# Where the tiles of a two-stage expert kernel start within a partition of SBUF

## The chip, the cores and the metric

The kernel runs on one core of a Trainium2 chip. The metric is the device time of one execution in microseconds (us): before the change the median of three runs is 1172.26 us (1172.18 to 1172.64).

## The reference

A causal convolution over 7 tokens, with softmaxed taps for each of 8 heads, then two feed-forward layers with different gates. All is float32.

```
w = softmax(weight)                                  # 8 heads x 7 taps
x = sum over k of w[head, k] * x_padded[token + k]   # x: 2 x 4096 tokens x 192
h = x @ w_in;  x = (h * clip(h + 3, 0, 6) / 6) @ w_out             # 192 -> 2048 -> 192
h = x @ w_in2; x = where(h > 0, h, exp(min(h, 0)) - 1) @ w_out2    # 192 -> 2048 -> 192
```

## The kernel before

The 8192 tokens are cut into 16 blocks of 512 columns, features on the partitions. Of each layer's 2048 hidden features, 128 make one *slot*: 2 layers x 16 blocks x 16 feature groups f = 512 slots. A slot has three steps.

- **First product** (`mm1`, L471 to L493): five matmuls of 512 columns put the sum h into one PSUM bank. To keep float32 accuracy with operands rounded to fp32r, weights and activations are split into a high and a low part, so `wi*h`, `wi*l` and `wi*r` (high, low, and both parts of the 64 features beyond 128) meet `opA`, `opB`, `opC` and `opD`.
- **Gate** (`gate`, `split_g`, L495 to L512): ScalarE makes u from h, VectorE makes g, ScalarE rounds it to `gh`, VectorE makes the rest `gl`.
- **Second product** (`mm2`, L516 to L532): five matmuls of `gh` and `gl` with slices of `wo` add into two PSUM banks over the 16 groups; the last slice of the five loads only 66 of 128 weight columns, save in the last group.

The second product runs LAG = 4 slots behind the first. The first 32 slots use all 128 rows of TensorE (`stream(ALL, ...)`, L793). After them two streams, one on partitions 0 to 63 and one on 64 to 127, are issued in turn, 8 matmuls apart (L805 to L812), so that two matmuls of 64 rows run side by side. In this form a slot has 9 first and 10 second matmuls.

Everything else is threaded between the slots by `run_jobs` (L578): decoding and splitting of the weights (`decode`, `split_w`), the convolution (`conv`), operand splits (`split_y`), sums and stores. Its meters count planned work and know nothing of addresses. Only the convolution of the first two blocks is done by TensorE (`taps_tensor`, L281): for k = 0 to 6 a plain float32 matmul of 256 columns reads the tile `xT` from 4k bytes past its start.

Tiles come from pools that are laid out in a partition one behind the other in the order of L90 to L97: `const`, `stage`, `xin`, `cv`, `tmp`, `gp`, `yp`, `op`. A tile's start is rounded up to 32 bytes only. As the small constants (`ident`, `taps` and the like) and the tiles of `cv` have odd sizes, the later pools start where these leave off. Of the starts the table gives the remainder in bytes, before the change; the tiles with several buffers have the same one in all.

| tile | size | start modulo 2048 | modulo 512 |
|---|---|---|---|
| `wi`, `wo` (weights) | 8192, 24576 | 128 | 128 |
| `opA` to `opD`, `gh`, `gl`, `g`, `u`, `xw`, `cw`, `y0`, `yr`, `s1` | 2048 | 1088 | 64 |
| `raw`, `y2`, `z` | 4096 | 1920 | 384 |
| `x_sb`, `xr_sb` | 2048, 1024 | 1920, 896 | 384 |
| `xT0` (two buffers) | 2096 | 1920, 1984 | 384, 448 |

One slot's weights of `wi` start at f x 512 bytes into the tile, those of `wo` at f x 1536 bytes plus 0, 512 or 1024. So modulo 2048 the weights of a matmul start at 128, 640, 1152 or 1664, by f.

Of the kernel before, what the change touches and what calls it, by code (L numbers as in the profile page):

```python
# [8 lines left out]
F32 = mybir.dt.float32  # L9
# [8 lines left out]
P = 128  # L18
# [37 lines left out]
def conv_moe_moe2(ctx: ExitStack, tc: tile.TileContext, x, weight, w_in1, w_out1, w_in2, w_out2, out):  # L56
# [19 lines left out]
    H, K = weight.shape  # L76
# [13 lines left out]
    const = ctx.enter_context(tc.tile_pool(name="const", bufs=1))  # L90
    stage = ctx.enter_context(tc.tile_pool(name="stage", bufs=3))
    xin = ctx.enter_context(tc.tile_pool(name="xin", bufs=2))
    cv = ctx.enter_context(tc.tile_pool(name="cv", bufs=1))
    tmp = ctx.enter_context(tc.tile_pool(name="tmp", bufs=2))
    gp = ctx.enter_context(tc.tile_pool(name="gp", bufs=LAG + 1))
    yp = ctx.enter_context(tc.tile_pool(name="yp", bufs=RA - 1))
    op = ctx.enter_context(tc.tile_pool(name="op", bufs=3))  # L97
    ps_h = ctx.enter_context(tc.tile_pool(name="ps_h", bufs=3, space=PSUM))
    ps_o = ctx.enter_context(tc.tile_pool(name="ps_o", bufs=5, space=PSUM))

    w_in = (w_in1, w_in2)
    w_out = (w_out1, w_out2)
    wi = [{n: const.tile([P, FF], F32R, name=f"wi{l}{n}") for n in ("h", "l", "r")} for l in range(2)]
    wo = [const.tile([P, NF, 2 * D], F32R, name=f"wo{l}") for l in range(2)]

    ident = const.tile([P, P], F32, name="ident")
    relay = const.tile([1, 1], F32, name="relay")
    three = const.tile([P, 1], F32, name="three")
    taps = const.tile([P, 2, K], F32, name="taps")


    def word(raw, i):
# [69 lines left out]


    def load_taps():
        raw = const.tile([H, K], F32, name="traw")
        nc.scalar.dma_start(raw, weight)
        e = const.tile([H, 2, P], F32, name="heads")
        nc.gpsimd.memset(e, 1.0)
        for part, pat, base in ((0, [[1, P]], 0), (1, [[0, 2], [1, R]], P)):
            v = e[:, part, :]  # L190
            nc.gpsimd.affine_select(out=v, in_=v, pattern=pat, compare_op=ALU.is_ge, fill=0.0,
                                    base=base, channel_multiplier=-G)
            nc.gpsimd.affine_select(out=v, in_=v, pattern=[[-st, n] for st, n in pat], compare_op=ALU.is_ge, fill=0.0,
                                    base=G - 1 - base, channel_multiplier=G)
        mx = const.tile([H, 1], F32, name="mx")
        vec.tensor_reduce(out=mx, in_=raw, axis=AX.X, op=ALU.max)
        vec.tensor_scalar(out=raw, in0=raw, scalar1=mx, scalar2=None, op0=ALU.subtract)
        ex = const.tile([H, K], F32, name="etap")
        act.activation(ex, raw, AF.Exp)
        sm = const.tile([H, 1], F32, name="sm")  # L200
        vec.tensor_reduce(out=sm, in_=ex, axis=AX.X, op=ALU.add)
        vec.tensor_scalar(out=sm, in0=sm, scalar1=1e-9, scalar2=None, op0=ALU.add)
        vec.reciprocal(sm, sm)
        vec.tensor_scalar(out=ex, in0=ex, scalar1=sm, scalar2=None, op0=ALU.mult)
        yield
        pt = ps_h.tile([P, 2, K], F32, name="pt", tag="h")
        for part in range(2):
            nc.tensor.matmul(pt[:, part, :], e[:, part, :], ex, start=True, stop=True)
        vec.tensor_copy(taps, pt)
        yield  # L210
# [471 lines left out]
    with tc.manual_schedule():  # L682
        tp, tr = load_taps(), transposes(0)
        make_identity(nc, ident)
        load_rows(0)
        next(tp)
        ahead(0)
        nc.gpsimd.memset(three, 3.0)
        next(tp)
        next(tr)  # L690
        next(tr)
        for k in range(K):
            vec.tensor_scalar(out=diag[k], in0=ident, scalar1=taps[:, 0, k:k + 1], scalar2=None, op0=ALU.mult)
        for _ in range(2):
            next(main)
        r = conv_r(0)
        while ready[0] < FIRST0:
            next(weights)
            next(r, None)
        drain(r)  # L700
        load_rows(1)
        drain(main)
# [6 lines left out]
    for b in range(2, NBLK):  # L709
        e = at[0, b, 0] - 2  # L710
        if b <= RA:
            t = at[0, b - 1, 0]
            if b > 2:
                t, e = t - 2, e + (b < RA)
            else:
                t += NF // 2
        else:
            t = at[0, b - 1, 0] - 8
            e = at[0, b - 1, NF - 1]
        job(feed(b), 1, t - 8, t - 7)  # L720
        job(whole(squares(b), conv(b)), 2 + CONV, t, e, WORK["conv"])
    for b in range(NBLK):
        e = at[1, b, 0]
# [120 lines left out]
```

## Time and profile before

| | |
|---|---|
| median of three runs | 1172.26 us |
| the profiled execution's own time | 1171.86 us |
| its span, first to last instruction | 1170.1 us |
| mean granted TensorE clock | 1.000 of full (2.4 GHz) |
| TensorE busy | 1159.8 us, 99% |
| VectorE busy | 918.7 us, 79% |
| ScalarE busy | 933.1 us, 80% |

The profile has one row per TensorE weight load (PEld) and per matmul (PE). Matmuls overlap in their pipeline, so the time that one costs is the distance between the starts of two, and not its own length. A plain float32 matmul leaves two records, an fp32r one leaves one.

### The profile page before, as it was taken

What the parts mean: (1) busy time and instruction counts of PE and PEld (TensorE: products, weight loads), DVE (VectorE), ACT (ScalarE), POOL (GpSimd) and SP (SyncE); (2) the same over time, 40 slices, a digit from 0 to 9 for tenths busy, and PEclk for the clock granted to TensorE, in tenths of its full rate; (3) what the DMA queues carried; (4) which work ended last, traced back from release to release, by engine and by line L of the source; (5) the groups of instructions that cost most, each with busy time, mean ns of one, the idle gap of its engine ahead of it and who ended that gap; (6) DMA issues with size and microseconds to landing.
All of it is one profiled execution on the core that took longest, in us unless ns stands there. A gap on an engine that the chain in (4) does not pass through costs nothing.

```text
span 1170.1 us, 25136 instructions
## 1 busy us (share of the span) xinstructions
PE 1159.8 (99%) x9507; PEld 1098.6 (94%) x9507; DVE 918.7 (79%) x1560; ACT 933.1 (80%) x1685; POOL 44.5 (4%) x490
## 2 busy tenths in 40 slices
PE   8999999999999999999999999999999999999998
PEld 6778999999999999999999999999999998878777
DVE  8997999988977968778686787968767666677765
ACT  6876777778878787887878778787786888888886
POOL 0000000000000000000000000000000000000000
PEclk9999999999999999999999999999999999999999
DMA  6422011010010100101000010100000000000001
GB/s 181 108 68 41 19 42 46 29 28 1 2 28 1 29 1 5 25 1 28 2 15 15 1 29 1 23 7 1 15 2 15 2 9 7 15 15 15 12 7 26
DMA packets 105370, 26.80 MB, mean 23 GB/s; under 512 B 96416, under 2 KB 104096, under 8 KB 105248
## 3 DMA queue, kind: packets, MB, share of 16 engines
q1 hardware_dynamic: 104960, 24.99, 10.1%
q8 instruction: 74, 1.21, 0.4%
q14 instruction: 48, 0.39, 0.1%
q10 hardware_dynamic: 288, 0.20, 0.1%
HBM read 18.87 MB, written 6.29 MB: 22 GB/s over the span
## 4 chain that ended last, share of the span: by engine, by line
PE 97%; DVE 1%; ACT 1%; issue 0%; ACTq 0%; DVEq 0%
PE p L530 50%; PE h L487 47%; DVE acc L50 0%; DVE xw L50 0%; ACT u L50 0%; DVE wi0r L50 0%; DVE cw L50 0%; ACT xw L50 0%; DVE diag L50 0%; ACT opC L50 0%; ACT L50 0%; DVE wo L50 0%; ACT gh L50 0%; ACT opD L50 0%; PE pso L432 0%
## 5 line engine op out<-in xcount | busy, mean ns | idle before, releaser
L530 PE MATMUL p<-gh,wo 64*128 64x512 f32 (+1 forms) x2978 | 625.5, 393 | 0.0
L50 DVE SCALAR_TENSOR_TENSOR g<-u,h 128x512 f32<-128x512 f32 x512 | 349.8, 683 | 214.7 <-ACT u L50 210.8
L530 PE MATMUL p<-gl,wo 64*128 64x512 f32 (+2 forms) x1985 | 503.2, 390 | 0.0
L530 PEld LDWEIGHTS p<-gh,wo 64*128 64x128 f32 (+1 forms) x2978 | 460.0, 185 | 15.5
L50 DVE TENSOR_TENSOR gl<-g,gh 128x512 fp32r<-128x512 f32 x512 | 349.9, 683 | 2.9 <-ACT gh L50 2.4
L50 ACT CAST gh<-g 128x512 fp32r<-128x512 f32 x512 | 311.2, 608 | 11.2 <-DVE g L50 11.0
L530 PEld LDWEIGHTS p<-gl,wo 64*128 64x128 f32 (+1 forms) x1985 | 309.4, 161 | 10.8 <-DVE gl L50 0.4
L50 ACT ACTIVATE u<-h,three 128x512 f32<-128x512 f32 x256 | 175.9, 687 | 120.4 <-PE h L487 116.9
L50 ACT ACTIVATE u<-h 128x512 f32<-128x512 f32 x256 | 152.6, 596 | 66.7 <-PE h L487 65.8
L487 PE MATMUL h<-opA,wi1h 64*128 64x512 f32 x512 | 194.9, 396 | 0.0
L487 PE MATMUL h<-opA,wi1l 64*128 64x512 f32 x512 | 194.6, 396 | 0.0
L487 PE MATMUL h<-opB,wi1h 64*128 64x512 f32 x512 | 192.3, 390 | 0.0
L487 PE MATMUL h<-opA,wi0h 64*128 64x512 f32 (+1 forms) x476 | 180.3, 396 | 0.5 <-ACT opA L50 0.4
L487 PE MATMUL h<-opA,wi0l 64*128 64x512 f32 (+1 forms) x476 | 179.9, 395 | 0.0
L487 PE MATMUL h<-opB,wi0h 64*128 64x512 f32 (+1 forms) x476 | 178.8, 391 | 0.0
L50 ACT ACTIVATE u<-u 128x512 f32<-128x512 f32 x256 | 161.8, 632 | 8.4
L487 PE MATMUL h<-opD,wi1r 64*128 64x512 f32 x384 | 147.1, 393 | 0.0
L487 PE MATMUL h<-opC,wi1r 64*128 64x512 f32 x384 | 146.3, 390 | 0.0
L487 PE MATMUL h<-opC,wi0r 64*128 64x512 f32 (+1 forms) x366 | 139.6, 391 | 0.6 <-ACT opC L50 0.6
L487 PE MATMUL h<-opD,wi0r 64*128 64x512 f32 (+1 forms) x366 | 140.2, 393 | 0.0
L50 DVE SCALAR_TENSOR_TENSOR acc<-xT,taps,acc 128x256 f32<-128x256 f32 (+1 forms) x180 | 105.4, 601 | 0.1
L487 PEld LDWEIGHTS h<-opA,wi1h 64*128 64x128 f32 x512 | 94.2, 184 | 6.6 <-DVE g L50 1.6
(89 smaller groups left out, 1215.4 us busy)
## 6 DMA issues: line engine op xcount, KB each, us to landing
raw<-in_moe_w_out_dram SPq DMA_DIRECT2D x16, 384.0 KB, 3.4
out_dram<-z SPq DMA_DIRECT2D x180, 32.0 KB, 1.6
raw<-in_moe_w_in_dram SPq DMA_DIRECT2D x7, 512.0 KB, 4.3
x_sq<-in_x_dram SPq DMA_DIRECT2D x112, 32.0 KB, 2.2
raw<-in_moe_w_in_dram SPq DMA_DIRECT2D x8, 256.0 KB, 4.0
xr_sq<-in_x_dram SPq DMA_DIRECT2D x56, 32.0 KB, 2.2
x_sb<-in_x_dram SPq DMA_DIRECT2D x4, 128.0 KB, 3.8
raw<-in_moe_w_in_dram SPq DMA_DIRECT2D x4, 128.0 KB, 3.5
```

The costliest lines, as they stand in the source:

```text
L50: return fn(*args, **kw)
L487: mm = nc.tensor.matmul(h, k, m[half], start=low and i == 0, stop=high and i == len(todo) - 1)
L530: nc.tensor.matmul(p[:n, cols], k[:, :n], m[half, cols], start=first and not end and k is not w0l, stop=last and end == 1 and cols.stop == NB)
```

## The change

No instruction is added, taken away or moved: each engine executes the same operations on the same tiles in the same order with the same waits. Two tiles that nobody uses are put ahead, of 384 bytes in `const` and of 320 bytes in `cv`, and the small constants go to a pool `few` of their own behind `op`.

```diff
     op = ctx.enter_context(tc.tile_pool(name="op", bufs=3))
+    few = ctx.enter_context(tc.tile_pool(name="few", bufs=1))
...
+    const.tile([P, 96], F32, name="gap0")
+    cv.tile([P, 80], F32, name="gap1")
     wi = [{n: const.tile([P, FF], F32R, name=f"wi{l}{n}") for n in ("h", "l", "r")} for l in range(2)]
     wo = [const.tile([P, NF, 2 * D], F32R, name=f"wo{l}") for l in range(2)]
 
-    ident = const.tile([P, P], F32, name="ident")
-    relay = const.tile([1, 1], F32, name="relay")
-    three = const.tile([P, 1], F32, name="three")
-    taps = const.tile([P, 2, K], F32, name="taps")
+    ident = few.tile([P, P], F32, name="ident")
+    relay = few.tile([1, 1], F32, name="relay")
+    three = few.tile([P, 1], F32, name="three")
+    taps = few.tile([P, 2, K], F32, name="taps")
```

The scratch tiles of `load_taps` (`traw`, `heads`, `mx`, `etap`, `sm`) move from `const` to `few` in the same way. The starts after the change:

| tile | start modulo 2048 | modulo 512 |
|---|---|---|
| `wi`, `wo` | 512 | 0 |
| `opA` to `opD`, `gh`, `gl`, `g`, `u`, `xw`, `cw`, `y0`, `yr`, `s1` | 0 | 0 |
| `raw`, `y2`, `z` | 512 | 0 |
| `x_sb`, `xr_sb` | 512, 1536 | 0 |
| `xT0` (two buffers) | 832, 896 | 320, 384 |

## Rows read from the trace of the kernel before

**Rows 1.** The page: busy time, share of the span, instructions of each engine.

```profile
PE 1159.8 (99%) x9507; PEld 1098.6 (94%) x9507; DVE 918.7 (79%) x1560; ACT 933.1 (80%) x1685; POOL 44.5 (4%) x490
```

**Rows 2.** The page: the chain that ended last, by engine and by line.

```profile
PE 97%; DVE 1%; ACT 1%; issue 0%; ACTq 0%; DVEq 0%
PE p L530 50%; PE h L487 47%; DVE acc L50 0%; DVE xw L50 0%; ACT u L50 0%; DVE wi0r L50 0%; DVE cw L50 0%; ACT xw L50 0%; DVE diag L50 0%; ACT opC L50 0%; ACT L50 0%; DVE wo L50 0%; ACT gh L50 0%; ACT opD L50 0%; PE pso L432 0%
```

**Rows 3.** Waits: the waiter, its releaser, us in total, times, the longest.

```profile
PE pt L208 <- DVE etap L50: 3.9, 1, 3.9
PE psx L244 <- DMA x_sb<-in_x_dram: 0.5, 1, 0.5
...
DVE g L50 <- ACT u L50: 210.8, 292, 3.5
ACT u L50 <- PE h L487: 182.7, 289, 2.2
```

**Rows 4.** Windows by stage (start, full rows, two streams, end), columns in line one.

```profile
core 0: us, PE busy (x) PEld busy (x) DVE busy (x) ACT busy (x) POOL busy (x), PEclk, DMA share, GB/s
0.00:31.00 31.00, 25.27 (x107) 20.14 (x107) 25.17 (x68) 22.07 (x52) 2.18 (x14) 1.00 0.68 174
31.00:103.00 72.00, 72.00 (x309) 56.47 (x310) 67.50 (x125) 56.48 (x102) 0.00 (x0) 1.00 0.29 74
103.00:1160.00 1057.00, 1057.00 (x9059) 1017.93 (x9059) 823.00 (x1363) 851.75 (x1527) 42.33 (x476) 1.00 0.08 15
1160.00:1170.10 10.10, 5.55 (x38) 4.04 (x34) 3.02 (x6) 2.78 (x6) 0.00 (x0) 0.95 0.13 40
```

**Rows 5.** Chain in order of time, full-row slots: start, length, what.

```profile
32.56 1.17 PE h L487 x5
...
34.88 1.17 PE h L487 x5
...
37.21 1.17 PE h L487 x5
...
46.52 1.17 PE h L487 x5
```

**Rows 6.** PE in order of time, one full-row slot: start, length, matmul.

```profile
60.31 0.40 PE L487 MATMUL h<-opA,wi0h 128*128 128x512 f32 x1
...
62.18 0.62 PE L530 MATMUL p<-gl,wo 128*128 128x512 f32 x2
62.64 0.40 PE L487 MATMUL h<-opA,wi0h 128*128 128x512 f32 x1
...
64.51 0.62 PE L530 MATMUL p<-gl,wo 128*128 128x512 f32 x2
64.97 0.40 PE L487 MATMUL h<-opA,wi0h 128*128 128x512 f32 x1
```

**Rows 7.** PE in order of time, convolution taps of block 1, in two windows.

```profile
17.40 1.24 PE L287 MATMUL psc<-xT,diag 128*128 128x256 f32 x5
...
17.40 5.99 PE L287 MATMUL psc<-xT,diag 128*128 128x256 f32 x27
```

**Rows 8.** PE in order of time, matmuls of 256 columns near the end.

```profile
1163.34 0.40 PE L530 MATMUL p<-gh,wo 64*128 64x256 f32 x2
...
1163.93 0.28 PE L530 MATMUL p<-gl,wo 64*128 64x256 f32 x1
```

More of the change, by code (lines that the diff above doesn't have):

```diff
@@ L184, in load_taps @@
     def load_taps():
-        raw = const.tile([H, K], F32, name="traw")
+        raw = few.tile([H, K], F32, name="traw")
         nc.scalar.dma_start(raw, weight)
-        e = const.tile([H, 2, P], F32, name="heads")
+        e = few.tile([H, 2, P], F32, name="heads")
         nc.gpsimd.memset(e, 1.0)
@@ L194, in load_taps @@
                                     base=G - 1 - base, channel_multiplier=G)
-        mx = const.tile([H, 1], F32, name="mx")
+        mx = few.tile([H, 1], F32, name="mx")
         vec.tensor_reduce(out=mx, in_=raw, axis=AX.X, op=ALU.max)
         vec.tensor_scalar(out=raw, in0=raw, scalar1=mx, scalar2=None, op0=ALU.subtract)
-        ex = const.tile([H, K], F32, name="etap")
+        ex = few.tile([H, K], F32, name="etap")
         act.activation(ex, raw, AF.Exp)
-        sm = const.tile([H, 1], F32, name="sm")
+        sm = few.tile([H, 1], F32, name="sm")
         vec.tensor_reduce(out=sm, in_=ex, axis=AX.X, op=ALU.add)
```

## The prediction

> **What bounds the kernel now.** I read four views. The page's busy times come first: TensorE is busy for 1159.8 of 1170.1 us, VectorE and ScalarE for about 80% [rows 1]. A busy share alone does not make a bound, so the chain that ended last is next. It runs through TensorE for 97%: half of that the second product (L530), nearly all of the rest the first (L487) [rows 2]. The waits point the same way. TensorE's longest is 3.9 us, once, at the start. VectorE waits 210.8 us for ScalarE's u, and ScalarE waits 182.7 us for a matmul's h, that is for TensorE [rows 3]. Last, the windows by stage: from 31 to 1160 us TensorE has no idle time at all, at a granted clock of 1.00. VectorE is busy for 823 of the 1057 us in the long stage and ScalarE for 852 [rows 4]. So only two things can move the time: the rate of a matmul, and the 41 us before and after (0 to 31 and 1160 to 1170).
>
> **The change part by part.** No instruction comes, goes or moves. What may change is the duration of an instruction, because its operands start elsewhere. I go through the places in order of their weight.
>
> *Matmuls at the full rate.* In the stage of full rows seven slot starts at 32.56, 34.88, ..., 46.52 give 13.96 us for six slots, 2.327 us each, or 232.7 ns for each of ten matmuls [rows 5]. In the two streams 9059 records in 1057 us are 116.7 ns apart, and as two run side by side this is 233.4 ns for a pair [rows 4]. Ideal for 512 columns at 2.4 GHz is 213.3 ns, so each costs 20 ns more, and the question of this case is whether these 20 ns hang on the addresses. The number of such units is 9059 / 2 + 309 = 4840 [rows 4]. One ns on each is therefore 4.84 us on the kernel.
>
> Three observations bear on it.
>
> First, the part of an address that is a multiple of 512 bytes makes no difference. From one slot to the next f changes, and with it the weights' start modulo 2048 goes through 128, 640, 1152 and 1664, while the moving operands stay at 1088. The slots still come 2.32 or 2.33 us apart each time [rows 5]. What the change alters for weights is a shift by 384 bytes, from remainder 128 to 0 modulo 512, and for moving operands from 64 to 0. Of that, only the part within 512 bytes is not tried out by the trace.
>
> Second, small misalignment costs next to nothing where the trace has it. The taps read `xT` from 4k bytes past its start, so from seven different places modulo 32. Their records are 215.9 ns apart: (5.99 - 1.24) / 22 [rows 7]. They stream two clocks per column, 256 columns in the 213.3 ns ideal, so the whole excess there, misalignment included, is 2.6 ns. The weights of these (`diag`) lie at 64 modulo 512. This is the nearest row to the question, at half the column rate.
>
> Third, the 20 ns follow other things. Five matmuls of 256 columns come 118 ns apart, (1163.93 - 1163.34) / 5 [rows 8], against 106.7 ideal: 11 ns excess for half the columns. And where the matmuls around a load of 66 columns stand, two take 0.46 us, while the eight others of the slot take 1.87 us [rows 6]: 230 against 233.75 ns. So the excess grows with the streamed columns and shrinks by about 7 ns for 62 columns less of weights. Neither row needs an address to explain it, but reads of weights and of moving data that disturb each other would fit the second.
>
> Bounds from these rows: at best the excess falls to that of the taps, 233.4 - 215.9 = 17.5 ns, times 4840 = 85 us less. At worst the part that goes with the weight load, 7 ns x 128 / 62 = 14 ns, is paid twice: 14 x 4840 = 68 us more. I take 0, by the taps, where starts off any multiple of 32 stay within 2.6 ns, and by the slots that repeat to 0.01 us for every position of the weights.
>
> The Trainium skill has a rule on each side here. "TensorE: Matmul & The Clock Gate", section "Wait — 56ns, not 53.3ns?", gives 215.7 ns between warm matmuls of 512 columns; this trace differs with 233.4 ns, and by that rule some 17.7 ns are there to be won by whatever causes them. "SBUF — State Buffer", section "Who interferes with whom", says that TensorE reads weights and moving data through independent ports and waits on nobody; by it the second bound cannot arise, though the 66-column rows above do not quite agree.
>
> *VectorE and ScalarE.* Their tiles move by the same few bytes. In the long stage they would have to grow by 1057 / 823 = 1.28 and 1057 / 852 = 1.24 before they set the rate [rows 4]. Their work is hidden behind TensorE there. If that cover went, each 1% on VectorE would be 8 us; the cover is 234 us deep. I count 0.
>
> *The start.* Up to 31 us VectorE is busy for 25.2 us, TensorE for 25.3 us of 31 [rows 4], and 5.7 us of TensorE are idle: 3.9 of them wait for the taps (`etap`) and 0.5 for the first `x_sb` [rows 3]. The tiles of the taps move from one odd place to another. Landing of `x_sb` and `raw` at 0 instead of 384 modulo 512 could move a transfer by a tenth or two. Bounds: 0.5 us less if the wait for `x_sb` goes, 0.5 us more if it doubles. I take 0.
>
> *The end.* Transposes, copies and one store from `z`: 10.1 us with 4.5 us of TensorE idle [rows 4]. The same order, the same size of transfer; within 0.3 us either way by the same reasoning, as an estimate. I take 0.
>
> *Sum.* The profiled execution took 1171.86 us, its span being 1170.1 and 1.76 us around it. 1171.86 + 0 = 1171.9; the median of the runs stands 0.4 us above that execution. On the scale of the median I forecast 1172.3 us.
>
> **The rivals.** A measurement of this kernel can tell about 0.2%, 2.3 us, from no change. On 4840 units that is 0.48 ns for a matmul: any address effect above half a nanosecond will be seen, and one rival or the other holds.
>
> *Rival 1, aligned moving reads stream faster.* Moving operands of 2048 bytes that start at 64 modulo 512 touch one more piece of any size from 128 to 2048 bytes than those at 0. If that piece, or the start in the middle of one, is behind the excess, it goes with the change. For: the excess grows with the columns [rows 8], and no matmul at the full rate in this trace has another remainder modulo 512, so it is not excluded. Against: one more piece would be a fixed cost, and half the columns have half of the excess; the taps don't show it [rows 7]. If the whole excess above the taps goes, the time is 1172.3 - 85 = 1087 us; if one piece in sixteen is saved (128 bytes of 2048), 20 / 17 = 1.2 ns x 4840 = 6 us, 1166 us. VectorE and ScalarE would fit into either: 823 and 852 us against 972 us at the shortest.
>
> *Rival 2, slower: weights and moving operands now meet.* Before, weights start at 128 and moving operands at 64 modulo 512; after, both start at 0. If reads at the same place modulo 512 disturb each other, loads and streams that begin together collide from their first bytes on. The place is every matmul of L487 and L530. For: a load of 66 columns instead of 128 makes the matmuls around it about 3.75 ns shorter each [rows 6], so a load does seem to cost the stream something. Against: within a load the weights pass through all places modulo 512 anyway (128 columns are 512 bytes). A quarter more of the 14 ns is 3.5 ns x 4840 = 17 us, 1189 us; the double is 1240 us. It decides from 0.48 ns on, a thirtieth of the 14 ns.
>
> *Rival 3, faster by fewer collisions.* The same mechanism with the other sign: before is the bad phase. A quarter less of 14 ns gives 1155 us, all of it 1104 us.
>
> **How the numbers follow.** No change holds 0.69: nothing in the trace reacts to an address, and what reacts does so to columns. Rival 1 gets 0.11, of which 0.04 for the small form, rival 3 0.06, together 0.17 faster. Rival 2 gets 0.14; in it I include a start that goes worse in some way by over 2.3 us, which the 0.5 us bound makes unlikely. The likeliest case alone lies between 1170.5 and 1173.8 (start and end together ±0.8 us, the runs' own spread of 0.5 us, and the 0.4 us between profile and median). To leave out no more than 2 in 10 the range takes in the small forms of the rivals: down to 1162, which holds the small form of rival 1, and up to 1180, a matmul longer by 1.6 ns. Faster 0.17, within 0.2% 0.69, slower 0.14.
>
> **What would show it.** Right: the slots of the full rows again 2.32 to 2.33 us apart, the 9059 records of the two streams in 1057 us, the 256-column matmuls again 118 ns apart. Rival 1: slots of less than 2.32 us, and the gain as large at the 66-column pairs as elsewhere. Rivals 2 and 3: the difference between pairs around 66-column loads and the others grows or shrinks, while the taps stay at 215.9 ns. An effect on VectorE or ScalarE would show in the mean durations of g, gl and gh without moving the end. The forecast is wrong if the long stage is longer or shorter than 1057 us by over 2 us.

## The result and the profile after

The changed kernel takes 1144.12 us (median of 5, 1143.75 to 1144.41) against 1172.26 us: ratio 0.9761, 95% interval 0.9750 to 0.9771. I had forecast no change, 1172.3 us, in a range of 1162 to 1180, so the time lies outside the range, on the side to which I gave 0.17.

The page of the changed kernel, busy time by engine, answers [rows 1]:

```profile
PE 1132.0 (99%) x9507; PEld 1020.9 (89%) x9507; DVE 918.7 (80%) x1560; ACT 929.7 (81%) x1685; POOL 44.7 (4%) x490
```

TensorE has lost 27.8 us of busy time with the same number of matmuls. VectorE is at 918.7 us as before, ScalarE 3.4 us lower. Two groups of the same page show how little their instructions care (between the bars: busy us and mean ns of one; behind them the idle time and its main cause):

```profile
L50 DVE SCALAR_TENSOR_TENSOR g<-u,h 128x512 f32<-128x512 f32 x512 | 350.0, 684 | 190.3 <-ACT u L50 185.3
...
L50 ACT CAST gh<-g 128x512 fp32r<-128x512 f32 x512 | 311.3, 608 | 13.4 <-DVE g L50 13.1
```

Before, the two means were 683 and 608 ns. What shrank is waiting: VectorE waits 185.3 us for u instead of 210.8, and ScalarE 155.5 us for h instead of 182.7 [rows 3].

The windows of the changed kernel, cut at the same places (columns as in [rows 4], stretch first):

```profile
0.00:31.00 31.00, 25.58 (x107) 20.35 (x107) 25.16 (x68) 22.05 (x52) 2.18 (x14) 1.00 0.65 174
31.00:103.00 72.00, 72.00 (x321) 57.85 (x323) 67.18 (x125) 56.45 (x102) 0.09 (x1) 1.00 0.29 74
103.00:1131.90 1028.90, 1028.72 (x9050) 938.80 (x9047) 823.17 (x1363) 848.38 (x1526) 42.42 (x475) 1.00 0.08 15
1131.90:1142.00 10.10, 5.66 (x38) 3.94 (x34) 3.14 (x6) 2.78 (x6) 0.00 (x0) 0.85 0.12 40
```

The start is the same: the first full slot of the chain begins at 32.57 us, before at 32.56 [rows 5]. So is the end, to 0.1 us: from the first 256-column matmul to the last instruction pass 6.65 us, before 6.76 [rows 8]. In the window of the full rows 321 matmuls go into 72 us instead of 309, and in the two streams a pair takes 2 x 1028.9 / 9050 = 227.4 ns instead of 233.4. At 4840 units, 6.0 ns are 29 us, which accounts for the whole difference of the spans, 1170.1 - 1142.0 = 28.1 us. The granted clock is 1.00 in both of these stages, before and after; in the last 10 us it is 0.85 instead of 0.95.

The slots in the chain of the changed kernel, in order of time (start, length, what), answer [rows 5]:

```profile
34.86 1.13 PE h L490 x5
36.00 1.13 PE p L533 x5
...
48.46 1.13 PE h L490 x5
```

Six slots take 13.60 us, 226.7 ns for each matmul, first product and second alike. The 66-column loads have stopped mattering: by the records all ten distances in a slot are 226 to 227 ns, where before the pairs around such a load took 230 and the rest 233.75 [rows 6]. One slot in order of time, as in [rows 6] (two take 0.45 us, eight 1.82):

```profile
59.63 0.39 PE L490 MATMUL h<-opA,wi0h 128*128 128x512 f32 x1
...
61.45 0.62 PE L533 MATMUL p<-gl,wo 128*128 128x512 f32 x2
61.90 0.39 PE L490 MATMUL h<-opA,wi0h 128*128 128x512 f32 x1
```

The taps and the 256-column matmuls have not changed, in the order of time of the changed kernel (two windows for the taps, as in [rows 7], then the end, as in [rows 8]):

```profile
17.40 1.24 PE L290 MATMUL psc<-xT,diag 128*128 128x256 f32 x5
...
17.40 5.99 PE L290 MATMUL psc<-xT,diag 128*128 128x256 f32 x27
...
1135.35 0.40 PE L533 MATMUL p<-gh,wo 64*128 64x256 f32 x2
...
1135.94 0.27 PE L533 MATMUL p<-gl,wo 64*128 64x256 f32 x1
```

215.9 and 118 ns again. So the change sped up matmuls of 512 columns at the full rate and nothing else. For the taps it could not have done otherwise by any effect of the distance between the two operands: `xT0` and `diag` both moved by 64 bytes modulo 256, so that distance is the same before and after.

### The profile page after: what moved, and what is told of

Its sections match the earlier page's. It is cut to its first block, busy times and chain, and to the rows that moved or that the text cites. A ratio compares the mean times of both kernels' runs of the same rounds, so it can differ in the third digit from the quotient of the medians.

```text
span 1142.0 us, 25136 instructions
## 1 busy us (share of the span) xinstructions
PE 1132.0 (99%) x9507; PEld 1020.9 (89%) x9507; DVE 918.7 (80%) x1560; ACT 929.7 (81%) x1685; POOL 44.7 (4%) x490
## 4 chain that ended last, share of the span: by engine, by line
PE 96%; DVE 2%; ACT 1%; issue 0%; ACTq 0%; DVEq 0%
PE p L533 50%; PE h L490 46%; ACT u L50 1%; DVE acc L50 0%; DVE xw L50 0%; ACT opC L50 0%; DVE g L50 0%; DVE gl L50 0%; ACT opD L50 0%; DVE wi0r L50 0%; DVE cw L50 0%; DVE diag L50 0%; ACT L50 0%; DVE wo L50 0%; ACT gh L50 0%
## 5 line engine op out<-in xcount | busy, mean ns | idle before, releaser
L533 PE MATMUL p<-gh,wo 64*128 64x512 f32 (+1 forms) x2978 | 598.5, 386 | 0.0
L50 DVE SCALAR_TENSOR_TENSOR g<-u,h 128x512 f32<-128x512 f32 x512 | 350.0, 684 | 190.3 <-ACT u L50 185.3
L533 PE MATMUL p<-gl,wo 64*128 64x512 f32 (+2 forms) x1985 | 481.5, 386 | 0.0
L533 PEld LDWEIGHTS p<-gh,wo 64*128 64x128 f32 (+1 forms) x2978 | 433.6, 184 | 28.9 <-ACT gh L50 0.2
L533 PEld LDWEIGHTS p<-gl,wo 64*128 64x128 f32 (+1 forms) x1985 | 292.0, 160 | 20.6 <-DVE gl L50 0.4
L490 PE MATMUL h<-opA,wi1h 64*128 64x512 f32 x512 | 182.6, 388 | 0.2
L490 PE MATMUL h<-opA,wi1l 64*128 64x512 f32 x512 | 182.2, 388 | 0.0
L490 PE MATMUL h<-opB,wi1h 64*128 64x512 f32 x512 | 181.5, 386 | 0.0
L490 PE MATMUL h<-opA,wi0h 64*128 64x512 f32 (+1 forms) x476 | 170.8, 389 | 0.5 <-ACT opA L50 0.3
L490 PE MATMUL h<-opB,wi0h 64*128 64x512 f32 (+1 forms) x476 | 170.4, 387 | 0.0
L490 PE MATMUL h<-opA,wi0l 64*128 64x512 f32 (+1 forms) x476 | 170.3, 387 | 0.0
```

The lines of the kernel that those rows point to most:

```text
L50: return fn(*args, **kw)
L490: mm = nc.tensor.matmul(h, k, m[half], start=low and i == 0, stop=high and i == len(todo) - 1)
L533: nc.tensor.matmul(p[:n, cols], k[:, :n], m[half, cols], start=first and not end and k is not w0l, stop=last and end == 1 and cols.stop == NB)
```

## The experiments

The theories: the start of the *moving* operand counts (my rival 1); the start of the *weights* counts; the *distance* between the two counts (rivals 2 and 3). All lengths in bytes; "distance" is the start of the weights minus that of the moving operand. The diffs of the layouts are against the changed kernel. The kernels of matmuls alone ran once each.

**One operand at a time.** `moving_only` leaves the weights at 128 modulo 512, distance 128:

```diff
-    const.tile([P, 96], F32, name="gap0")
-    cv.tile([P, 80], F32, name="gap1")
+    cv.tile([P, 176], F32, name="gap1")
```

> Weights back at 128 modulo 512 bytes, as before; moving operands, g and sums at 0, as after. If the start of the moving operand alone sets the rate of a matmul: 1144 us, 226.7 ns from matmul to matmul in the full-row slots. If the start of the weights alone does: 1172 us, 233.3 ns. If what counts is the distance between the two (64 bytes before, 0 after, here 128): neither is bound to come out; any other time than these two speaks for it, and equal starts are tried by the run both64.

Measured: 1169.58 us, ratio 0.9982 (0.9973 to 0.9991). `weights_only` leaves the moving operands at 1088, distance 192 modulo 256, by putting the small constants but `ident` back into `const`:

```diff
-    cv.tile([P, 80], F32, name="gap1")
+    cv.tile([P, 32], F32, name="gap1")
...
-    taps = few.tile([P, 2, K], F32, name="taps")
+    taps = const.tile([P, 2, K], F32, name="taps")
```

> Weights at 0 modulo 512 bytes, as after; moving operands, g and sums at 1088 modulo 2048 (64 modulo 512), as before. Start of the moving operand alone: 1172 us, 233.3 ns a matmul. Start of the weights alone: 1144 us, 226.7 ns. Distance: it is 64 as before but with the other sign, so 1172 us if the sign does not count.

Measured: 1163.57 us, ratio 0.9934 (0.9916 to 0.9953). The two gains, 2 and 8 us against the kernel before, don't add up to 28, and neither start alone has it. `both64` pushes the whole changed layout on by 64 bytes:

```diff
-    const.tile([P, 96], F32, name="gap0")
+    const.tile([P, 112], F32, name="gap0")
```

> The whole of the changed layout pushed on by 64 bytes: weights and moving operands both start at 64 modulo 512. Distance theory (equal starts are fast): 1144 us, 226.7 ns. Start of either operand against a multiple of 128 to 512: 1172 us, 233.3 ns, or something between if each has a share.

Measured: 1144.04 us, ratio 0.9761 (0.9745 to 0.9778). Both operands start off every multiple of 128, at 64 modulo 512, and the whole gain is there. This refutes rival 1 and the weights' alignment, and with them the multiples of 512 and 2048 that the change is made of: what it did was to make two starts equal.

**A table of starts.** `grid` is a kernel of matmuls alone:

```
for m in range(0, 512, 32):
    for w in range(0, 512, 32):
        ten matmuls: 128 weight columns from w, or w + 2048, 512 moving columns from m
```

> Matmuls alone: 128 rows, 512 columns of fp32r, 128 columns of weights loaded for each, ten in a row for every pair of starts in steps of 32 bytes modulo 512 (name m<moving>w<weights>); the rest of the computation is left out. The start-to-start distance should be 233 ns at m64w128 and 227 ns at m0w0. Moving start alone: it changes with m and not with w. Weights alone: with w and not with m. Distance: it is constant where m - w is.

Start-to-start means in ns, worked out from the records, from the second of each ten to the first of the next ten (four rows of 16, nine columns of 16):

```
         w=0    32    64    96   128   160   192   224   256
m=0    227.7 232.7 233.1 233.3 233.0 233.6 230.0 233.3 230.1
m=32   233.3 230.1 232.6 233.1 233.3 233.0 233.6 230.0 233.3
m=64   229.9 233.3 230.1 232.6 233.1 233.3 233.0 233.6 229.9
m=256  230.1 232.6 233.1 233.3 233.0 233.6 229.9 233.3 230.1
```

Along the diagonals the value stays, and it repeats after 256 in both directions: the distance modulo 256 counts. The expected 227 at distance 0 is there only in the first series, which followed 40 matmuls of its own kind. In the others it is 230, because a series first goes through some seven uneven distances (at m32w32: 236, 224, 231, 236, 228, 233, 230, then 227 and 227). So `fine` has 40 in a row.

> Matmuls alone again, 40 in a row so that a steady state shows; the rest of the computation is left out. d<n>: start of the weights minus start of the moving operand in bytes, 512 columns, 128 weight columns, in steps of 16 and 4; n<columns>k<weight columns>d<n>: other sizes; bf<n>: bf16 operands; half<n>: two streams of 64 rows, one 8 matmuls behind. Theory that weight reads and moving reads hinder each other by their distance modulo 256: d0 226.7 ns, d64 233, d128 233; the part above d0 shrinks with the weight columns (at 32 columns a quarter of the 6.7 ns, about 228.5); bf16 reads half the bytes and shows little of it. Rival, that a weight load costs a fixed time by its address whatever its size: d64 stays at 233 with 32 weight columns. What is left of the excess at d0 (13.4 ns over 213.3): if it belongs to the moving stream alone it halves with 256 columns (113.3 ns) and stays with 32 weight columns; if it belongs to the change of weights it stays 13 ns (120 ns).

PE in order of time in `fine` (start, length, matmul; the start of the next series minus this one, over 40, is the mean):

```profile
43.91 9.24 PE L39 MATMUL d0x<-M,W 128*128 128x512 f32 x40
52.98 9.45 PE L39 MATMUL d4x<-M,W 128*128 128x512 f32 x40
62.27 9.39 PE L39 MATMUL d8x<-M,W 128*128 128x512 f32 x40
...
108.69 9.49 PE L39 MATMUL d64x<-M,W 128*128 128x512 f32 x40
118.02 9.44 PE L39 MATMUL d80x<-M,W 128*128 128x512 f32 x40
127.30 9.53 PE L39 MATMUL d96x<-M,W 128*128 128x512 f32 x40
136.67 9.49 PE L39 MATMUL d112x<-M,W 128*128 128x512 f32 x40
...
210.98 9.30 PE L39 MATMUL d240x<-M,W 128*128 128x512 f32 x40
220.11 9.25 PE L39 MATMUL n512k128d0x<-M,W 128*128 128x512 f32 x40
...
387.61 8.81 PE L39 MATMUL bf0x<-Mb,Wb 128*128 128x512 bf16 x39
```

Distance 0: 226.8 ns. Four bytes off: 232.3. Distance 64, as before the change: 233.3; 96, the worst: 234.3; 240: 228.3. At distance 128 one series took 233.4 and another 232.5, so differences of under 1 ns are not read. In steady state (the mean of the last 20 distances) the two-stream form comes to 226.7 too at distance 0, and there at 240 as well. bf16 does not care (215 to 216 ns between neighbouring records at each of the four distances). So far as expected; the sizes were not: 66 weight columns at distance 0 took 235.7 ns in steady state, and 32 columns 231.6 at 0 and at 64. The excess does not shrink with the load, and both theories of its size fail.

**Does the table carry over?** Two layouts of the full kernel, at distances 256 and 96:

```diff
-    const.tile([P, 96], F32, name="gap0")
-    cv.tile([P, 80], F32, name="gap1")
+    const.tile([P, 160], F32, name="gap0")     # dist96: 120
+    cv.tile([P, 16], F32, name="gap1")         # dist96: 56
```

> Weights at 256 modulo 512 bytes, moving operands at 0. If what counts is the distance modulo 256, as the table of starts has it: 1144 us, 226.7 ns in the full-row slots. If the weights must lie at a multiple of 512, or both at the same remainder modulo 512: slower, 1160 to 1172 us.

> Weights at 96 modulo 256, moving operands at 0: the worst distance of the table, 234.3 ns in steady state against 226.7 at 0. If the table carries over to the kernel: 1144 + 4840 x 7.6 ns = 1181 us, slower than the kernel before. If in the kernel only distance 0 is special and all others are alike: 1165 to 1172 us.

`dist256`: 1143.76 us, ratio 0.9760 (0.9745 to 0.9774), as the distance modulo 256 has it. `dist96`: 1177.05 us, ratio 1.0043 (1.0026 to 1.0059), slower than before by 5 us. The sign was right and the size about right (+33 us against the changed kernel, 37 expected). The chain of `dist96` in order of time:

```profile
32.56 1.17 PE h L490 x5
...
46.58 1.17 PE h L490 x5
```

14.02 us for six slots, 233.7 ns a matmul.

The table can be held against the first two layouts too, `moving_only` at distance 128 and `weights_only` at 192. By distance 0, 192, 128, 64 and 96 `fine` has 226.7, 228.8, 233.3, 233.3 and 234.3 ns in steady state, and the full kernel takes 1144, 1164, 1170, 1172 and 1177 us: the same order. The size does not carry over at 192: 2.1 ns on 4840 units would give 1154 us as an estimate, and `weights_only` took 1163.6 (1162.0 to 1167.6, a wider spread than the other layouts have). Its chain in order of time:

```profile
33.13 1.15 PE h L490 x5
...
46.89 1.15 PE h L490 x5
```

That is 229.3 ns a matmul in the full rows, near the table. The two streams of the same execution take 232.4 ns a pair; why they are slower at this distance is not known.

**Whose distance, and does a neighbour matter?** `pair` alternates the moving start and gives the weights either their own operand's start or the one that streams while they load; `mix` has a 66-column load in every tenth.

> Matmuls alone; the rest of the computation is left out. The moving start alternates between 0 and s (64 or 128) from one matmul to the next. own<s>: a matmul's own weights lie at distance 0 from its own moving operand, so at distance s from the one that streams while they are loaded. while<s>: the weights lie at distance 0 from the operand that streams while they are loaded, so at s from their own. If the load and the stream that runs meanwhile hinder each other: while64 and while128 settle at 226.7 ns, own64 and own128 at 229 to 234. If a matmul's own pair counts: the other way round. mix<d>: 128 weight columns but 66 in every tenth, as in the second product: mix0 226.7 if, as in the changed kernel, the shorter load does not disturb; mix64 233.

PE in order of time in `pair`:

```profile
44.61 9.42 PE L35 MATMUL own64x<-M,W 128*128 128x512 f32 x40
53.87 9.41 PE L35 MATMUL while64x<-M,W 128*128 128x512 f32 x40
63.12 9.30 PE L35 MATMUL own128x<-M,W 128*128 128x512 f32 x40
72.26 9.36 PE L35 MATMUL while128x<-M,W 128*128 128x512 f32 x40
81.46 22.90 PE L35 MATMUL mix0x<-M,W 128*128 128x512 f32 x100
104.20 23.43 PE L35 MATMUL mix32x<-M,W 128*128 128x512 f32 x100
```

Neither pairing reaches 226.7: 231.5 (`own`) and 231.3 (`while`) for 64, 228.5 and 230.0 for 128. The run does not decide which of the two distances counts. `mix0` does settle (226.7 ns after the first dozen), `mix64` takes 232.7 in steady state, as in the slots before the change.

The full kernel's counterpart is `wo64`, with distance 0 in the first product and 64 in the second:

```diff
     wi = [{n: const.tile([P, FF], F32R, name=f"wi{l}{n}") for n in ("h", "l", "r")} for l in range(2)]
+    const.tile([P, 16], F32, name="gap2")
     wo = [const.tile([P, NF, 2 * D], F32R, name=f"wo{l}") for l in range(2)]
-    cv.tile([P, 80], F32, name="gap1")
+    cv.tile([P, 64], F32, name="gap1")
```

> The changed layout, but the weights of the second product (wo, half of all matmuls) pushed on by 64 bytes: distance 0 in the first product, 64 in the second. If each matmul pays for its own distance: half of the gain is left, 1158 us. If a pace of 226.7 ns only settles where all neighbours are at distance 0, as the slow start of each series in the table and the runs own64 and while64 suggest: more than half is lost, 1162 us or above.

Measured: 1166.87 us, ratio 0.9957 (0.9942 to 0.9972). Of 28 us only 5 are left, where half of the matmuls still have distance 0. The chain in order of time:

```profile
32.56 1.16 PE h L491 x5
...
46.48 1.16 PE h L491 x5
```

13.92 us for six slots, 232.0 ns a matmul; by the records of the full rows the first product, at distance 0, takes 231.5 ns a matmul. So a matmul does not pay for its own distance alone: five in a row at distance 0 do not reach 226.7 ns here, and in the series above it took some seven.

**What the excess is made of.** `sizes` varies the moving columns and the weight columns, and moves both operands together:

> Matmuls alone, 40 in a row; the rest of the computation is left out. n<columns>d<distance>: at distance 0, 512 and 256 columns both cost 13.3 ns above the columns at 2.4 GHz; if that is a fixed cost of a matmul with its load, 448, 384 and 320 columns cost it too (200, 173.3, 146.7 ns); if 512 is a lucky length, they cost 17 to 20. k<weight columns>d<distance>: if the load's reads disturb the stream, 2 weight columns bring the matmul near 215 to 217 ns at either distance; if each change of weights costs a fixed time, it stays at 227 to 233. at<m>: both operands moved by 4 to 20 bytes at distance 0: 226.7 if only the distance counts.

PE in order of time in `sizes`:

```profile
166.08 4.97 PE L34 MATMUL n256d0x<-M,W 128*128 128x256 f32 x40
170.88 4.88 PE L34 MATMUL n256d64x<-M,W 128*128 128x256 f32 x40
175.60 4.91 PE L34 MATMUL n256d128x<-M,W 128*128 128x256 f32 x40
...
202.87 9.32 PE L34 MATMUL k2d0x<-M,W 128*2 128x512 f32 x40
212.03 9.43 PE L34 MATMUL k2d64x<-M,W 128*2 128x512 f32 x40
221.31 9.43 PE L34 MATMUL k16d0x<-M,W 128*16 128x512 f32 x40
...
313.75 9.31 PE L34 MATMUL k112d0x<-M,W 128*112 128x512 f32 x40
322.91 9.23 PE L34 MATMUL k112d64x<-M,W 128*112 128x512 f32 x40
331.97 9.23 PE L34 MATMUL k128d0x<-M,W 128*128 128x512 f32 x40
...
369.13 9.48 PE L34 MATMUL at16x<-M,W 128*128 128x512 f32 x40
378.45 9.56 PE L34 MATMUL at20x<-M,W 128*128 128x512 f32 x40
```

Distance 0 is not best for every length. At 256 columns it costs 120.0 ns and distance 64 costs 118.0, so no gain was to be had from the 256-column matmuls at the kernel's end; the loss of 2 ns that this table has for them does not show in those six, which are fewer than a series takes to settle. At 320 columns all four distances take 146.6 to 146.7 in steady state, and 448 columns take 206.7 at distance 0, 202.2 at 64 and 200.0 at 240. Above the columns at 2.4 GHz, distance 0 costs the same 13.3 ns at 256, 320, 384 (173.3 ns) and 512 columns, as a fixed cost would have it, but 20 ns at 448 and 32 at 192 (111.6 ns). Two weight columns still cost 229 and 232 ns: the rival of a cost by the size of the load falls. But the fast distance hangs on the number of weight columns: with 112 of them it is 64 that settles at 226.7 ns, and 0 takes 229.0; with 96 they take 228.3 and 230.0; with 66 `fine` has 235.7, 235.0 and 228.0 at distances 0, 64 and 128. So equal starts are the fast place for 512 moving and 128 weight columns, and no run shows a rule for the others.

And `at16`, distance 0 with both starts at 16, takes 233.3 in steady state, while starts at 32 (the end of m32w32 in `grid`) and at 64 (`both64`) come to 227 and 226.7: starts finer than 32 count for themselves. My expectation for `at` was wrong.

`reads` asks whether it is the reading at all, by letting an operand read one element over and over:

```
wsame: weights t[:, d:d+1].to_broadcast([P, 128])    msame: moving t[:, 0:1].to_broadcast([P, 512])
```

> Matmuls alone, 512 columns of fp32r and 128 weight columns, 40 in a row; the rest of the computation is left out. plain<d>: as in the table, weights at distance d. wsame<d>: all weight columns read one element, so the load reads one place only. msame<d>: all moving columns read one element. bothsame<d>: both. If the two reads hinder each other in SBUF: with either of them in one place the dependence on d goes or changes, and where the moving read has one place only the time falls below 226.7, towards the 215.9 of the taps. If the cost is in changing the weights in the array, whatever is read: all stay at 226.7 or above with the moving data from one place too.

PE in order of time in `reads`:

```profile
45.37 9.23 PE L38 MATMUL plain0x<-M,W 128*128 128x512 f32 x40
54.44 9.41 PE L38 MATMUL wsame0x<-M,W 128*128 128x512 f32 x40
63.69 8.91 PE L38 MATMUL msame0x<-M,W 128*128 128x512 f32 x40
72.43 8.91 PE L38 MATMUL bothsame0x<-M,W 128*128 128x512 f32 x40
81.17 9.50 PE L38 MATMUL plain64x<-M,W 128*128 128x512 f32 x40
90.51 9.40 PE L38 MATMUL wsame64x<-M,W 128*128 128x512 f32 x40
99.75 8.90 PE L38 MATMUL msame64x<-M,W 128*128 128x512 f32 x40
108.50 8.91 PE L38 MATMUL bothsame64x<-M,W 128*128 128x512 f32 x40
```

With the moving data from one place a matmul takes 218.6 ns at every distance, though weights load as before. With the weights from one place it takes 231.2, 231.1 and 231.6 ns at distances 0, 64 and 128, so nothing that can be read is left of the dependence. So the dependence needs both reads to walk through SBUF, and in this run the change of weights itself costs at most the 5 ns between 218.6 and the ideal 213.3. This is as far as the runs show the cause: the time of an fp32r matmul depends on where its two reads start relative to each other. That the moving stream and the weight load read SBUF in each other's way is the reading that fits, and is argued, not shown. It is not the whole story: at distance 0 a load that reads one place (231.2 ns) is worse than one that walks (226.7). No run streams fp32r columns without a new load for each matmul, so how much of the 13.3 ns that are left above the ideal belongs to the moving stream alone is open; in proportion to its columns it is not. Why 32-byte starts and some lengths matter is open too.

## Why the prediction was wrong

- *What bounds the kernel* held: only the matmul rate moved the time, and the 0 for VectorE, ScalarE, start and end was right in effect.
- The step that failed is "I take 0, by the taps". I named the taps the nearest row and noted that they stream at half the column rate, and then used them as if that did not matter. The taps took 215.9 ns before and after, but their own distance did not change, so they could not tell; nor do their small misalignments tell, since they stream 256 columns in two clocks each and `sizes` has the effect change with the number of columns. The term that I put at 0 measured -6.0 ns on each of 4840 units (233.4 to 227.4 ns in the two streams, 232.7 to 226.7 in the full rows).
- The first observation, that slots repeat to 0.01 us at every position of the weights, was true, and I read too much into it. It tries multiples of 512 only, and the effect repeats after 256. I did write that the part within 512 is not tried out, and should have let that stand as an unknown with bounds of +68 and -85 us, instead of 0.69 for no change.
- The third observation was a clue: a row in which a shorter weight load changed the distance between matmuls by 3.75 ns showed that the load matters to the pace. *Rival 3*, faster by fewer collisions, had the sign right, and so was what I had named to show it: the difference around the 66-column loads went and the taps stayed. Its mechanism fits, as far as `reads` goes. Its "quarter less" and "all" gave 1155 and 1104 us; the measured 6.0 ns is 0.43 of the 14 ns. I gave it 0.06, by no row. That the hindrance is in proportion to the weight columns, from which I had the 14 ns and with it the upper bound, is wrong: 2 columns take 229 to 232 ns (`k2`), and 66 in every matmul at distance 64 take 235.0 against 233.3 with 128 (`fine`). The shorter load in that row was no saving of its own.
- *Rival 1* is refuted by `both64`. *Rival 2* had it the wrong way round: equal starts are the fast place for 128 weight columns. A slower place exists elsewhere, `dist96` being 5 us slower than before.
- The Trainium skill, "SBUF — State Buffer", section "Who interferes with whom", has TensorE's two reads on independent ports. `fine` does not fit with that: the distance between the two starts alone takes a matmul from 226.7 to 234.3 ns. "TensorE: Matmul & The Clock Gate", section "Wait — 56ns, not 53.3ns?", gives 215.7 ns; bf16 in `fine` agrees (215.8 ns between neighbouring records), fp32r with both operands read in full took 226.7 at best.

## What to carry to other kernels

Where TensorE bounds a kernel with fp32r operands and a new load of 128 weight columns for every matmul of 512 columns, give weights and moving operands the same start modulo 256 bytes, at a multiple of 32, for all matmuls that follow each other; here that alone is worth 2.4%. For other sizes measure first: 112 weight columns were faster at distance 64 than at 0, and of four distances 256 and 448 moving columns were slowest at 0. Absolute alignment to 512 or 2048 is not needed, and half a fix gave 5 of 28 us. When a trace has no variation in a quantity that the change moves, say that the effect is unknown and give it its bounds; a row from another rate does not stand in for it.

## What the runs showed of the hardware

- fp32r matmuls of 512 columns with a load of 128 columns each take 226.7 ns at distance 0 modulo 256 and 228.3 to 234.3 at the other multiples of 16 (`fine`), and 237.8 at distance 0 with both starts at 4 (`sizes`).
- With 112 weight columns distance 64 takes 226.7 ns and distance 0 takes 229.0 (`sizes`).
- At distance 0 the pace is settled by what went before: after a series at another distance some seven matmuls take between 224 and 236 ns before they run evenly at 226 and 227 (`grid`). Five at a time between five at distance 64 stay at 231.5 (`wo64`).
- Reading the moving operand from one place brings 218.6 ns (`reads`); bf16 takes 215.8 (`fine`).
